# One block's x transposed by DMA instead of by TensorE, and its neighbour's V loaded from GpSimd's queue, in a fused chunk attention and squared-ReLU feed-forward kernel

## The chip, the cores and the metric

The kernel runs on one core of a Trainium2 chip. The metric is the device time of one execution in microseconds (us); a kernel's figure is the median over its runs. Besides the plain times there is one profiled execution, whose trace gives the engines' instructions in order of time.

## The reference

Attention inside chunks of 64 tokens, for 8 batches, 8 heads, 576 tokens and head size 64, and after it a feed-forward layer with a squared ReLU on the 4608 rows of 512 that the attention gives.

```python
# q, k, v: (8, 8, 576, 64) float32, cut into chunks of 64 tokens
scores = scale * np.matmul(q_c, k_c.transpose(0, 1, 2, 4, 3))
attn = exp(scores - max) ; attn = attn / (sum(attn) + 1e-09)
x = np.matmul(attn, v_c)              # then laid out as (4608, 512)
h = np.maximum(x @ w_in, 0.0)         # w_in: (512, 2048)
out = (h * h) @ w_out                 # w_out: (2048, 512), out float32
```

## The kernel before

Tokens are worked in 18 groups of 256 (four chunks each), and two groups make a block of 512 tokens: nine blocks, 0 to 8. Block 4 is groups 8 and 9, block 5 is groups 10 and 11, block 6 is groups 12 and 13. The whole order of the work is written out by hand: every step is put into a numbered slot, and the engines execute what they are given in that order.

**Attention of a group.** q and k of a group are loaded into a staging buffer by three DMAs on SyncE's queue (SP), two for k and one for q (`qk_pieces`, L266 and L279). `C`, made of `CQ` and `CK` (L449, L454), casts them to bfloat16 into `qkb`, on GpSimd for block 5. `TD` (`transpose_qk_dma`, L460) transposes `qkb` into `qkT` with one DMA on SP. `SC` (`scores`, L483 and L494) does 32 small matmuls and one Exp on ScalarE. `AV` (`values`, L510) multiplies with V, in two tiles, and VectorE divides by the row sums and writes the tile of `x` (L442, L443). V of a group is loaded by DMAs on SP (`v_pieces`, L308 for the even heads, L312 for the odd ones): five for group 10, four for group 11. `XT` (`transpose_x`) brings x into `xT`, tokens along the free dimension: with eight TensorE transposes into a PSUM bank and a copy by ScalarE (L540, L545), or, for the blocks in `X_BY_DMA`, with one DMA transpose on SP (L535). PSUM banks for attention are handed out in turn by `att_bank`, two of them in this stage.

**Feed-forward.** Blocks 0 to 3 have a plain first product, `ffn_in`: 16 slots, each with four matmuls of 128x512 (L579), a ReLU on ScalarE (L590) and a square on VectorE (L598), or on ScalarE for slots 3, 10 and 14. The squares are the pieces of `gT`. From block 4 on the first product is done by a Strassen-like scheme of seven products per quarter block (`quad_step`, L657, steps A1, B2, A6, C5, A7, C3, A4), which needs four sums of x, `x_sums` 0 to 3, called e1 to e4 below. VectorE forms them (L614). e1 is made of two parts of group 8 alone; e2 is e1 plus a part of group 9, e3 is e2 minus a part of group 9, and e4 is made of parts of both. A1 reads e1, A6 reads e2, C5 reads e3, A4 reads e4.

The second product (`ffn_out`) has the same kind of scheme, with the differences d4, d5, d2 and d3 of `gT` pieces formed by VectorE (L614, written to `w_st`). For block 3 it is a generator: d4 is formed in two halves in input slots 14 and 15, and then come 14 output steps of eight matmuls (L780): two of the product p2, which reads `gT` itself, two of p1, which reads d4, then two with d5, and so on. d5 is formed after the third output step.

**Around the change.** Block 3's input stage (`j == 3` in the loop over `QUADS`) holds, beside its 16 x 4 matmuls: `SC` of groups 8 and 9 in slot 2, `AV` of group 8 in slot 6 and of group 9 in slot 10, the loads for block 5 (one per slot in slots 0 to 10), the casts of group 10 in slot 11, the cast of q of group 11 and `TD` of group 10 in slot 13, `XT` of group 8 in slot 13 and of group 9 in slot 15. The first `LEAD` = 4 output steps of block 3 then run before the first quarter of block 4, with `between[n]` executed after n of them: `CK` and `TD` of group 11 and one more load before the first, one load after each of the next three, and the x sums. Then block 4's quarters interleave with the other ten output steps, `SC` of group 10 at 1.5, `SC` of group 11 at 3.5, and the four `AV` tiles of block 5 at 4.5, 6, 7.5 and 10 (a unit is one pair of products).

SP executes its DMA instructions in order. In the program as built, each DMA of SP also waits until the one eight before it on SP has landed, and the same holds on GpSimd's queue (eight semaphores in turn on either). GpSimd's queue holds, in order: the casts for block 5, a store of an output tile (L809), then two squares of block 4's products (L676).

Of the kernel before, what the change touches and what calls it, by code (L numbers as in the profile page):

```python
# [144 lines left out]
def kernel(  # L145
# [34 lines left out]


    FIRST_DMA_T = 4
    X_BY_DMA = (6, 7, 8)
    QUADS = 4
    LEAD = 4

# [60 lines left out]
    def runs(g):  # L247

        for t in range(2):
            (b, s), (b1, s1) = chunks[g][2 * t:2 * t + 2]  # L250
            if b == b1:
                yield t, 0, 2 * CH, b, s
            else:
                yield t, 0, CH, b, s
                yield t, CH, CH, b1, s1
# [48 lines left out]
    def v_pieces(g):  # L304

        even, odd = [], []
        for t, p, m, b, s in runs(g):
            even.append(lambda t=t, p=p, m=m, b=b, s=s: nc.sync.dma_start(  # L308
                out=v_even[g % NV][p:p + m, t, :, 0:D],
                in_=v[b, 0::2, s:s + m, :].rearrange("h s d -> s h d")))  # L310
        for n, p, m, b, s in odd_loads[g]:
            odd.append(lambda n=n, p=p, m=m, b=b, s=s: nc.sync.dma_start(  # L312
                out=v_odd[n % NO][p:p + m, :, 0:D],
                in_=v[b, 1::2, s:s + m, :].rearrange("h s d -> s h d")))
        if g < 2:
            yield from [even[0], *odd[:-1], even[1], odd[-1]]
        else:
            yield from even + odd

    def go(pieces):  # L320
        for f in pieces:
            f()
# [604 lines left out]
    def pieces(grps):  # L927
        for g in grps:
            yield from qk_pieces(g)
        for g in grps:  # L930
            yield from v_pieces(g)
# [72 lines left out]
    for j in range(QUADS):  # L1004
        grps, nxt, far = blocks[j], blocks[j + 1], blocks[j + 2]
        plan = {}

        def at(slot, f, *x):
            plan.setdefault(slot, []).append((f, x))

        if j == 0:
            loads, go_slots = pieces(far), range(17)
            at(28, summed(b11_p_b21, b11, b21))
            for slot, f in ((24, TA), (27, SC), (29, AV), (31, XT)):
                at(slot, f, nxt[0])
            at(31, TQ, nxt[1])
            at(31, TK, nxt[1])
            at(31, summed(b22_m_b21, b22, b21, ALU.subtract))
            phases = [first_ffn_in, ffn_out_by_ft(0)]
        elif j == 1:  # L1020
            loads, go_slots = itertools.chain(*map(qk_pieces, far)), range(26, 48)
            for slot, f in ((3, SC), (6, AV), (12, XT)):
                at(slot, f, grps[1])
            for i, g in enumerate(nxt):
                for slot, f in ((16 + 4 * i, C), (21 + 4 * i, TD), (36 + i, SC), (38 + 2 * i, AV),
                                (41 + 2 * i, XT)):
                    at(slot, f, g)
            for i, g in enumerate(far):
                at(36 + 4 * i, C, g)
                at(42 + 3 * i, TD, g)  # L1030
            at(2, summed(b12_p_b21, b12, b21))
            at(12, summed(b11_m_b12, b11, b12, ALU.subtract))
            at(20, summed(b12_p_b22, b12, b22))
            out_j = ffn_out(1)
            for i in (20, 27, 29, 31):
                at(i, lambda: next(out_j)())
            phases = [ffn_in(1, [(0, 256, FT_ORDER), (256, 256, FT_ORDER)]), out_j]
        else:
            out_j = ffn_out(j)
            for i in (14, 15):  # L1040
                at(i, lambda: next(out_j)())
            phases = [ffn_in(j, [(0, BT, range(n_ft))])]
            if j == 2:
                loads, go_slots = itertools.chain(*map(v_pieces, nxt), pieces(far)), [
                    *range(16), *range(27, 36)]
                slots = {SC: (6, 10), AV: (12, 22), XT: (15, 28), CQ: (20, 22), CK: (21, 24), TD: (24, 26)}
                for f in (CQ, CK, TD):
                    for i, g in enumerate(far):
                        at(slots[f][i], f, g)
                phases.append(out_j)  # L1050
            else:
                loads, go_slots = pieces(far), range(11)
                at(11, C, far[0])
                at(13, CQ, far[1])
                at(13, TD, far[0])
                slots = {SC: (2, 2), AV: (6, 10), XT: (13, 15)}
            for f in (SC, AV, XT):
                for i, g in enumerate(nxt):
                    at(slots[f][i], f, g)
            if j == 2:  # L1060
                for i, f in enumerate((summed(a21_p_a22, a21, a22),
                                       summed(a12_m_a21, a12, a21, ALU.subtract),
                                       summed(a11_p_a21, a11, a21))):
                    at(1 + 2 * i, f)
        slot = 0
        for phase in phases:
            for _ in phase:
                if slot in go_slots:
                    for f in loads:
                        f()  # L1070
                        break
                for f, x in plan.get(slot, []):
                    f(*x)
                slot += 1
        assert all(x < slot for x in plan), (j, slot, sorted(plan))
        if j < QUADS - 1:
            go(loads)
# [19 lines left out]
    for j in range(QUADS, n_blk):  # L1097
        if j == QUADS:
            n = 14 - LEAD
            slots = [1 + 19 * i // n for i in range(n)]  # L1100
            assert len(slots) == n
        else:
            slots = [s for s in range(4, 20) if s % 16 not in NO_OUT]
            start = 3
        if j == QUADS:
            g = blocks[QUADS + 1][1]
            between = {0: [(CK, (g, nc.scalar.copy)), (TD, (g,))]}
            for n in (0, 1, 2, 3):
                between.setdefault(n, []).append((load, (1, loads)))
            for n in (2, 2, 2, 3):  # L1110
                between.setdefault(n, []).append((x_sums, (QUADS, len([1 for z in between.values() for y in z if y[0] is x_sums]))))
            for f, x in between.get(0, []):
                f(*x)
            for i in range(LEAD):
                next(out_j)
                tock()
                for f, x in between.get(i + 1, []):
                    f(*x)
        else:
            outs[j - 1] = ffn_out(j - 1)  # L1120
            at(j, start, lambda j=j: next(outs[j - 1])())
        for s in slots:
            plan.setdefault(("out", 16 * (j - QUADS) + s), []).append(outs[j - 1])

        if j + 1 < n_blk:
            S0, V0, V1, X0 = ((1.5, 3.5), (4.5, 7.5), (6, 10), (8.5, 12)) if j == QUADS else (
                (1.5, 7), (3.5, 8), (5, 9.5), (5.5, 10)) if j == QUADS + 1 else (
                (0.5, 7), (2, 8), (3.5, 9.5), (3.5, 10)) if is_whole(blocks[j + 1][0]) else (
                (3.5, 9.5), (5, 11), (7, 12), (8, 13))
            for i, g in enumerate(blocks[j + 1]):  # L1130
                at(j, S0[i], SC, g)
                at(j, V0[i], AV0, g)
                at(j, V1[i], AV1, g)
                at(j, X0[i], XT, g)
            if j + 2 == n_blk:
                at(j, 22, check_sums)
                at(j, 25.5, count_bad)
            for i, s in enumerate((13.5, 16 if j == n_blk - 3 else 15, 17.5, 18)):
                at(j, s, x_sums, j + 1, i)
        if j == QUADS:  # L1140
            for s in range(4):
                at(j, 4 * s + 2, w_sums_in_place, s)
            assert next(loads, None) is None
        if j + 2 < n_blk:
            more = pieces(blocks[j + 2])
            if j == n_blk - 3:

                for s, n in ((0, 1), (1, 1), (2, 1), (8.5, 3), (13, 5), (15, 2), (15.5, 2)):
                    at(j, s, load, n, more)
            else:  # L1150
                for s in range(0, 16):
                    at(j, s, load, 1 if is_whole(blocks[j + 2][0]) else 2, more)
            for i in range(2):
                at(j, (9, 10 if j == QUADS else 13)[i], C, blocks[j + 2][i])
                at(j, ((9.5, 14.5) if j == n_blk - 3 else (12, 13.5))[i], TD, blocks[j + 2][i])
# [66 lines left out]
```

## Time and profile before

| | us |
|---|---|
| runs of the kernel | 277.05, 277.80, 279.23 (median 277.80) |
| the profiled execution | 276.91 |
| its span in the trace | 275.1 |
| VectorE busy | 199.2 |
| ScalarE busy | 168.3 |
| GpSimd busy | 89.6 |
| median issue to landing, q of a group (512 KB) | 5.6 |
| the same, V for 128 rows (128 KB) | 3.9 and 3.6 |

The profiled execution is 1.8 us longer than its span, the part that lies outside of the trace's first and last instruction, and 0.9 us below the median of the three runs. The granted TensorE clock is full in every stretch of the span. In the listings, PE is TensorE's matmuls, PEld its weight loads, DVE VectorE, ACT ScalarE, POOL GpSimd, SP SyncE, and SPq what SP spends on issuing DMAs.

### The profile page before, as it was taken

The numbers are of one execution on the slowest core, as the hardware profiler recorded it, in microseconds if no ns is written. First come the engines' busy times: TensorE is split into PE (matmuls) and PEld (weight loads), VectorE is DVE, ScalarE is ACT, GpSimd is POOL, SyncE is SP. The second block draws the span as 40 slices with busy tenths as digits, with TensorE's granted clock in tenths as the row PEclk, the third lists the DMA queues.
The fourth block names the chain that finished last, engine by engine and source line by source line (L and its number), as shares of the span: only waits on it lengthen the run. The fifth ranks groups of instructions, "written<-read, shape, count | busy, mean of one in ns | idle before, by whom it ended". The sixth has DMA issues, their size and how long they took to land.

```text
span 275.1 us, 7923 instructions
## 1 busy us (share of the span) xinstructions
PE 264.9 (96%) x3261; PEld 203.4 (74%) x3261; DVE 199.2 (72%) x365; ACT 168.3 (61%) x300; POOL 89.6 (33%) x122
## 2 busy tenths in 40 slices
PE   2999999999999999999999999999999999999995
PEld 2764445888774588447878888888888888888884
DVE  1457514999538592499989998799779877994752
ACT  1657614894458883877678765565746665756430
POOL 2048834240360012040245224551643212331600
PEclk9999999999999999999999999999999999999999
DMA  7999999999999999999999999697999530220223
GB/s 216 262 352 389 361 332 270 339 213 172 262 210 218 238 234 218 275 223 178 228 236 197 218 238 194 103 220 196 244 187 224 123 76 2 99 55 7 71 83 114
DMA packets 136056, 55.60 MB, mean 202 GB/s; under 512 B 104273, under 2 KB 131921, under 8 KB 136017
## 3 DMA queue, kind: packets, MB, share of 16 engines
q1 hardware_dynamic: 133248, 46.54, 74.0%
q0 software_dynamic: 2624, 8.39, 9.6%
q8 instruction: 26, 0.43, 0.6%
q10 hardware_dynamic: 144, 0.13, 0.1%
q14 instruction: 14, 0.11, 0.1%
HBM read 36.70 MB, written 9.44 MB: 168 GB/s over the span
## 4 chain that ended last, share of the span: by engine, by line
PE 87%; DMA 4%; SPq 3%; DVE 3%; ACT 1%; issue 1%; ACTq 0%; DVEq 0%
PE ps_ffn L657 22%; PE ps_out L780 22%; PE ps_ffn L579 17%; PE ps_ffn L780 14%; PE ps_ffn L901 5%; PE ps_att L510 3%; PE ps_att L540 2%; DMA vo_sb<-in_v_dram 2%; PE ps_att L483 2%; DMA xT<-x 2%; DVE gT L598 2%; SPq L266 1%; SPq L308 1%; SPq L312 1%; DVE x L443 1%; ACT e L494 1%
## 5 line engine op out<-in xcount | busy, mean ns | idle before, releaser
L579 PE MATMUL ps_ffn<-xT,w_in_bf 128*128 128x512 bf16 (+1 forms) x328 | 57.8, 333 | 0.0
L780 PEld LDWEIGHTS <-w_st 128*128 128x128 bf16 x512 | 48.9, 98 | 6.6 <-DVE w_st L614 0.5
L665 DVE CUSTOM_DVE_ANT_0 relu<-ps_ffn,w_st 128x512 f32<-128x512 f32 x60 | 39.3, 684 | 13.0 <-PE ps_ffn L657 11.6
L579 PEld LDWEIGHTS <-w_in_bf 128*128 128x128 bf16 x328 | 31.2, 98 | 21.6 <-POOL w_in_bf L334 0.2
L598 DVE TENSOR_TENSOR gT<-relu 128x256 bf16<-128x256 bf16 (+2 forms) x68 | 34.1, 537 | 17.8 <-ACT relu L590 17.3
L590 ACT ACTIVATE relu<-ps_ffn 128x256 bf16<-128x256 f32 (+2 forms) x82 | 39.4, 501 | 9.4 <-PE ps_ffn L579 8.6
L657 PE MATMUL ps_ffn<-qk_st,w_in_bf 128*128 128x256 bf16 x240 | 35.3, 273 | 0.1
L657 PEld LDWEIGHTS <-w_in_bf 128*128 128x128 bf16 x320 | 30.7, 98 | 4.1 <-issue 0.3
L809 POOL DMA_DIRECT2D out_dram<-o_sb x24 | 17.6, 733 | 43.6 <-DVE o_sb L614 23.3
L780 PEld LDWEIGHTS <-gT 128*128 128x128 bf16 x296 | 28.6, 98 | 3.3
L780 PE MATMUL ps_out<-w_out_bf,w_st 128*128 128x256 bf16 x240 | 30.8, 273 | 0.0
L699 ACT ACTIVATE w_st<-ps_ffn 128x512 f32<-128x512 f32 x20 | 11.9, 597 | 29.6 <-PE ps_ffn L657 29.6
L443 DVE TENSOR_TENSOR x<-ps_att,recs 128x512 bf16<-128x512 f32 x36 | 24.9, 692 | 1.2
L657 PEld LDWEIGHTS <-qk_st 128*128 128x128 bf16 x240 | 22.6, 98 | 3.2 <-DVE qk_st L614 0.3
L657 PE MATMUL ps_ffn<-xT,qk_st 128*128 128x256 bf16 x160 | 23.9, 273 | 0.0
L676 POOL TENSOR_TENSOR qk_st<-relu 128x512 bf16<-128x512 f32 x10 | 10.3, 1034 | 41.6 <-DVE relu L665 38.1
L494 ACT ACTIVATE e<-ps_att 128x1024 bf16<-128x1024 f32 x18 | 18.3, 1025 | 8.5 <-PE ps_att L483 8.5
L676 POOL TENSOR_TENSOR gT<-relu 128x512 bf16<-128x512 f32 x10 | 10.3, 1033 | 35.4 <-DVE relu L665 30.5
L449 POOL CAST qkb<-qk_st 128x1024 bf16<-128x1024 f32 x12 | 13.0, 1082 | 14.9 <-DMA qk_st<-in_q_dram 14.9
L674 ACT ACTIVATE gT<-relu 128x512 bf16<-128x512 f32 x28 | 17.7, 631 | 0.0
L780 PE MATMUL ps_ffn<-w_out_bf,w_st 128*128 128x256 bf16 x144 | 17.7, 273 | 0.0
L614 DVE TENSOR_TENSOR w_st<-gT,w_st 128x1024 bf16<-128x1024 bf16 x26 | 16.8, 682 | 0.0
(92 smaller groups left out, 428.7 us busy)
## 6 DMA issues: line engine op xcount, KB each, us to landing
qk_st<-in_q_dram SPq DMA_DIRECT2D x16, 512.0 KB, 5.6
out_dram<-o_sb POOLq DMA_DIRECT2D x28, 256.0 KB, 3.9
qk_st<-in_k_dram SPq DMA_DIRECT2D x24, 256.0 KB, 5.6
ve_sb<-in_v_dram SPq DMA_DIRECT2D x32, 128.0 KB, 3.9
w_st<-in_moe_w_in_dram SPq DMA_DIRECT2D x8, 512.0 KB, 5.9
w_st<-in_moe_w_out_dram SPq DMA_DIRECT2D x8, 512.0 KB, 5.5
vo_sb<-in_v_dram SPq DMA_DIRECT2D x24, 128.0 KB, 3.6
qk_st<-in_k_dram SPq DMA_DIRECT2D x4, 512.0 KB, 5.8
```

The costliest lines, as they stand in the source:

```text
L443: nc.vector.tensor_tensor(out=x, in0=o[:, :, :, 0:D], in1=rec.to_broadcast([128, 2, n, D]), op=ALU.mult)
L494: nc.scalar.activation(out=e_out, in_=s_in, func=AF.Exp, scale=scale)
L579: nc.tensor.matmul(out=h[:, 0:n], lhsT=w_in_bf[:, dt, ft * 128:(ft + 1) * 128], rhs=xT[:, c // 128:(c + n) // 128, dt, :], start=(dt == 0) ...
L590: nc.scalar.activation(out=rl[:, 0:n], in_=h[:, 0:n], func=AF.Relu)
L598: nc.vector.tensor_tensor(out=dst, in0=src, in1=src, op=ALU.mult)
L614: nc.vector.tensor_tensor(out=out, in0=in0, in1=in1, op=op)
L657: nc.tensor.matmul(out=bank[:, f * GT:(f + 1) * GT], lhsT=a[:, dt, ft * 128:(ft + 1) * 128], rhs=b[:, :, dt, :], start=(first and f == 0 a ...
L665: nc.vector._custom_dve(TENSOR_ADD_SAT, out=out, in0=in0, in1=in1, s0=BIG, s1=0.0)
L674: engine.activation(out=dst, in_=r, func=AF.Square)
L676: engine.tensor_tensor(out=dst, in0=r, in1=r, op=ALU.mult)
L780: nc.tensor.matmul(out=out_ps, lhsT=lhsT, rhs=b[:, i, :], start=(first and i == 0 and (last or t == 0)), stop=(i == HF - 1), skip_group_ch ...
L809: dma.dma_start(out=out[t0:t0 + GT, col:col + HD].rearrange("(t p) d -> p t d", p=128), in_=o_sb.rearrange("p (t d) -> p t d", d=HD))
```

## The change

Three edits.

1. Block 4 joins the blocks whose x is transposed by DMA on SP. `XT` of group 8 moves from slot 13 to slot 8 of block 3's input stage and `XT` of group 9 from slot 15 to slot 11; `TD` of group 10 moves from slot 13 to slot 12.
2. V of groups 10 and 11 (block 5) is issued by GpSimd on its own queue, no longer by SP: the five of group 10 together in slot 13, behind the cast of q of group 11; the four of group 11 where their issues stood before, through `between`. The loads of slots 0 to 5 are the six of q and k, as before.
3. Of the four x sums of block 4, e1 stays after the second output step of block 3; e2 and e3 move to after the third, where e4 already was. On VectorE this puts them behind the two instructions of d5.

In the built program TensorE has 32 instructions fewer (16 weight loads and 16 transposes, L540), ScalarE two copies fewer (L545), SP nine V loads fewer and two transposes more, GpSimd nine DMA issues more.

```diff
     FIRST_DMA_T = 4
-    X_BY_DMA = (6, 7, 8)
+    V_BY_GPSIMD = (10, 11)
+    X_BY_DMA = (4, 6, 7, 8)
...
     def v_pieces(g):
 
         even, odd = [], []
+        dma = nc.gpsimd if g in V_BY_GPSIMD else nc.sync
         for t, p, m, b, s in runs(g):
-            even.append(lambda t=t, p=p, m=m, b=b, s=s: nc.sync.dma_start(
+            even.append(lambda t=t, p=p, m=m, b=b, s=s: dma.dma_start(
                 out=v_even[g % NV][p:p + m, t, :, 0:D],
                 in_=v[b, 0::2, s:s + m, :].rearrange("h s d -> s h d")))
         for n, p, m, b, s in odd_loads[g]:
-            odd.append(lambda n=n, p=p, m=m, b=b, s=s: nc.sync.dma_start(
+            odd.append(lambda n=n, p=p, m=m, b=b, s=s: dma.dma_start(
...
             else:
-                loads, go_slots = pieces(far), range(11)
+                loads, go_slots = pieces(far), range(6)
                 at(11, C, far[0])
+                at(12, TD, far[0])
                 at(13, CQ, far[1])
-                at(13, TD, far[0])
-                slots = {SC: (2, 2), AV: (6, 10), XT: (13, 15)}
+                at(13, lambda: go(itertools.islice(loads, 5)))
+                slots = {SC: (2, 2), AV: (6, 10), XT: (8, 11)}
...
-            for n in (2, 2, 2, 3):
+            for n in (2, 3, 3, 3):
                 between.setdefault(n, []).append((x_sums, (QUADS, ...
```

The branch that `XT` of block 4 now takes is already in the kernel before:

```python
        if g // 2 in X_BY_DMA:
            nc.sync.dma_start_transpose(out=dst, in_=x.rearrange("p t h a d -> p (t h a d)"))
            return
```

## The prediction

> **What bounds the kernel now.** I read the page first, then the chain of waits, then the timeline of block 3's input stage and of the first 20 us behind it. The page:
>
> ```profile
> span 275.1 us, 7923 instructions
> PE 264.9 (96%) x3261; PEld 203.4 (74%) x3261; DVE 199.2 (72%) x365; ACT 168.3 (61%) x300; POOL 89.6 (33%) x122
> PE 87%; DMA 4%; SPq 3%; DVE 3%; ACT 1%; issue 1%; ACTq 0%; DVEq 0%
> ```
>
> TensorE (PE) is busy for 96% of the span and carries 87% of the chain, so removed TensorE work should shorten the kernel, unless TensorE then waits at the same place. The chain of waits through the stage that is changed (start, length, what):
>
> ```profile
> 115.70 1.90 DVE gT L598 x3
> ...
> 119.28 2.78 DVE gT L598 x3
> 122.21 0.70 DVE x L443
> 122.96 0.62 PE ps_att L540 x8
> ```
>
> From 115.70 on VectorE carries the chain, and the eight transposes of group 8 (L540) come off it at 122.96: their PSUM bank is free only when x of group 9's first tile has been read. One square among these is slow; the first row is VectorE's groups from 120.8 to 121.6, the second GpSimd's cast of k of group 10 in the timeline:
>
> ```profile
> L598 DVE TENSOR_TENSOR gT<-relu 128x512 bf16<-128x512 f32 x1 | 1.5, 1519 | 0.0
> 120.21 1.30 POOL L454 CAST qkb<-qk_st 128x1024 bf16<-128x1024 f32 x1 [0.74 <-DMA qk_st<-in_k_dram]
> ```
>
> The timeline of the same place, TensorE first and then VectorE (start, length, instructions; idle before it in brackets):
>
> ```profile
> 120.08 2.76 PE L579 MATMUL ps_ffn<-xT,w_in_bf 128*128 128x512 bf16 x12
> 123.42 1.89 PE L579 MATMUL ps_ffn<-xT,w_in_bf 128*128 128x512 bf16 x8
> 125.14 0.61 PE L540 MATMUL ps_att<-ident,x 128*128 128x128 bf16 x8
> 125.59 1.91 PE L780 MATMUL ps_out<-w_out_sum,gT 128*128 128x256 bf16 x16
> 127.34 1.94 PE L780 MATMUL ps_out<-w_out_bf,w_st 128*128 128x256 bf16 x16
> 129.11 0.60 PE L657 MATMUL ps_ffn<-qk_st,w_in_bf 128*128 128x256 bf16 x4
> ```
>
> ```profile
> 123.05 0.69 DVE L443 TENSOR_TENSOR x<-ps_att,recs 128x512 bf16<-128x512 f32 x1
> 123.66 1.89 DVE L598 TENSOR_TENSOR gT<-relu 128x512 bf16<-128x512 f32 x3
> 125.46 0.68 DVE L614 TENSOR_TENSOR w_st<-gT 128x1024 bf16<-128x1024 bf16 x1
> 126.31 0.69 DVE L598 TENSOR_TENSOR gT<-relu 128x512 bf16<-128x512 f32 x1 [0.17 <-ACT relu L590]
> 127.04 0.69 DVE L614 TENSOR_TENSOR w_st<-gT 128x1024 bf16<-128x1024 bf16 x1
> 127.65 0.42 DVE L614 TENSOR_TENSOR qk_st<-xT 128x512 bf16<-128x512 bf16 x1
> 128.98 1.28 DVE L614 TENSOR_TENSOR w_st<-gT,w_st 128x1024 bf16<-128x1024 bf16 x2
> ```
>
> VectorE has one idle piece of 0.17 us there. The row at 127.04 is the second half of d4, and ends at 127.73. Product p1 (127.34) reads that half from its fifth matmul on: p1 takes 129.11 - 127.34 = 1.77 us for 16, so the fifth starts at 127.34 + 4 x 0.111 = 127.78. TensorE is 0.05 us behind VectorE already.
>
> **Transposes removed from TensorE and ScalarE.** Eight matmuls take (125.14 - 123.42) = 1.72 us up to the second eight transposes, which fill 125.14 to 125.59 (0.45 us). Without transposes slots 14 and 15 follow slot 13 directly: 120.08 + 12 x 0.215 = 122.66, and 1.72 us later, at 124.4, p2 starts instead of at 125.59. TensorE gains 1.2 us by then: 0.3 us of wait and twice 0.45 us.
>
> That gain meets VectorE. Its instructions are the same and in the same order up to e1, and those up to 126.1 had no idle time to lose. The last ReLU comes earlier (its matmuls end at 124.4), so only the 0.17 us before 126.31 goes, 0.24 us with the gap in the issue. The second half of d4 ends at about 127.5, and p1's fifth matmul, which TensorE could reach at 124.4 + 1.75 + 0.44 = 126.6, waits until 127.55. Twelve matmuls later, 127.55 + 1.33 = 128.9, comes A1, at 129.11 before: **0.2 us gained** of 1.2. ScalarE's two copies had nothing behind them that sets the end but this ReLU, and so are worth nothing more.
>
> The slow square (1.52 us, where the three from 123.66 take 0.63 each) lies beside that cast. The loads of q and k and the cast stay where they are, so I leave this time in.
>
> **x sums.** VectorE after the change: d4 to 127.5, e1 (0.42) to 127.9, d5 (1.28) to 129.2, e2 and e3 to 130.1. TensorE needs e1 at 128.9, d5 at 129.7, e2 for A6 at 130.6 (0.2 us before its old 130.86). Each is early by 0.5 to 1 us, the total is the same: zero, as long as the xT of group 9 lands by 129.2.
>
> **The two transposes on SP.** SP's rows, and the time that each kind of transpose takes to issue and to land (min/median/max):
>
> ```profile
> 118.21 1.73 SPq L279 DMA_DIRECT2D qk_st<-in_k_dram  x2
> 124.36 5.15 SPq L460 DMA_TRANSPOSE qkT<-qkb  x2
> L535 SPq DMA_TRANSPOSE xT<-x x6: 1233/1555/2757, 162.7 to 223.9; - x6
> DMA to landing us min/median/max: 3.0/4.6/5.5
> L460 SPq DMA_TRANSPOSE qkT<-qkb x14: 1317/3058/4518, 61.7 to 206.3; - x14
> DMA to landing us min/median/max: 4.5/6.1/8.5
> ```
>
> x of group 8 is ready at 119.28 (the chain) and SP free at 118.21 + 1.73 = 119.94: landing at 122.9 to 125.4, e1 reads it at 127.5. x of group 9 is ready at 123.05 + 0.69 = 123.74: its transpose is issued at 123.8 and lands at 126.8 to 129.3, at 128.4 by the median; e2 reads it at 129.2. Both hidden, the second by 0.8 us. Behind it on SP stands `TD` of group 10, whose casts were done long before: issued at 123.8 + 1.55 = 125.4, 1.0 us later than before. `TD` of group 11 follows at up to 128.4 (before, the second of the two rows waited for a cast that the copies on ScalarE held up). Who waits for them:
>
> ```profile
> 131.39 0.45 PE L483 MATMUL ps_att<-qkT 64*64 64x64 bf16 x32
> 134.05 0.45 PE L483 MATMUL ps_att<-qkT 64*64 64x64 bf16 x32
> 136.28 0.22 PE L510 MATMUL ps_att<-ve_sb,e 64*64 64x65 bf16 x2
> 140.07 0.22 PE L510 MATMUL ps_att<-ve_sb,e 64*64 64x65 bf16 x2
> ```
>
> Scores of group 10 now come at 131.2, 5.8 us after the issue; of group 11 at 133.8, 5.4 us after it. By the minimum (4.5) both are hidden, by the median (6.1) they cost 0.3 and 0.7 us, by the maximum 3. Here the V loads no longer stand ahead of `TD` on SP, so I take a landing of 5 to 5.5 us and a cost of zero, with 0 to 3.1 us for the range.
>
> **V on GpSimd.** Nine issues behind the cast of q of group 11, ahead of a store and a square:
>
> ```profile
> 122.01 1.04 POOL L449 CAST qkb<-qk_st 128x1024 bf16<-128x1024 f32 x1 [0.50 <-DMA qk_st<-in_q_dram]
> 131.50 0.71 POOL L809 DMA_DIRECT2D out_dram<-o_sb  x1 [8.45 <-DVE o_sb L614]
> 131.71 1.28 DVE L614 TENSOR_TENSOR w_st<-gT 128x1024 bf16<-128x1024 bf16 x2
> 135.83 1.04 POOL L676 TENSOR_TENSOR qk_st<-relu 128x512 bf16<-128x512 f32 x1 [3.62 <-DVE relu L665]
> L809 POOL DMA_DIRECT2D out_dram<-o_sb x24: 707/738/751, 69.9 to 239.0; - x24
> DMA to landing us min/median/max: 2.2/3.6/6.0
> ```
>
> No V load is issued there before. The nearest row is a store, 0.74 us for 256 pieces of 1 KB. A V load has 512 pieces of 256 B (two of the nine have half): by bytes no more than the store, by pieces 1.48 us. Nine take 6.6 us or 7 x 1.48 + 2 x 0.74 = 11.8 us, from 123.05 to between 129.7 and 134.9; even then the store (0.71) ends at 135.6, before the square's 135.83. The fifth load is issued by 129.0 and lands by 135.0 at the slowest row (6.0); `AV` needs it at 136.1. The ninth lands by 139.4 in the same way, group 11's `AV` is at 139.9. Cost zero, thinly covered at the slow end. If an issue held up VectorE as the cast did (0.9 us), the four to six issues that lie before d4's end would cost some 4 to 5 us; but VectorE beside a store (131.71, two in 1.28 us) is not slowed at all, and a V issue is nearer to a store than to a cast.
>
> SP loses the nine issues (five of them fill 119.94 to 124.36) and gains two of 1.55 us, so block 6's loads start 1 to 3 us earlier. One wait later on could profit, the 0.20 us before this:
>
> ```profile
> 206.62 0.61 PE L657 MATMUL ps_ffn<-qk_st,qk_st 128*128 128x256 bf16 x4 [0.20 <-DVE qk_st L614]
> ```
>
> I count half of it. Sum: -0.2 - 0.1 = -0.3 us, a span of 274.8. The profiled execution takes 276.91, 1.8 outside its span, and lies 0.9 below the median 277.8. Median to median: **277.5**.
>
> **Rivals.** *TensorE's whole gain arrives:* 277.8 - 1.2 - 0.1 = 276.5. It needs VectorE's 12 us from 115.70 to 127.73 to shrink by 1 us, for instance if the cast no longer meets the square (0.9 us). Against it: nothing in the change moves that cast.
>
> *Transposes late, the slow side:* `TD` of groups 10 and 11 land more than 5.8 and 5.4 us after their issue, because V now runs at the same time from another queue instead of ahead of them, and two more transposes are in flight. TensorE executes in order, so each tenth beyond is lost. 6.1 us gives 277.5 + 0.7 = 278.2; 8.5 us gives 277.5 + 3.1 = 280.6 (the second wait holds the first). For it: the median of 14 landings is already beyond the point. Against it: the scores rows at 131.39 and 134.05 show no wait for a DMA, though V stood ahead of both on the same queue. [...]
>
> [...]
>
> That the transposes stay on TensorE is no rival: the built program has 16 fewer.
>
> **Numbers.** The forecast has 0.56, TensorE's whole gain 0.12, late transposes 0.25, starved V 0.07. A median of this kernel can't be told from no change within about 1%, 275.0 to 280.6. The forecast and the whole gain lie inside but for spread (runs of one kernel span 277.05 to 279.23): faster 0.04. Slower takes starved V and a quarter of the late transposes: 0.13. Same 0.83. The range goes from the whole gain with 0.3 of spread, 276.2, to late transposes at 279.8.
>
> **What would show it.** Right: no L540 after 115, p2 near 124.4, a wait of 0.9 us in p1 for VectorE, A1 near 128.9, scores of groups 10 and 11 without a wait for DMA, V issues of 0.7 to 1.5 us on POOL. Wrong: L443 or L598 ending earlier than in the rows above (more gain), PEld waiting on qkT at L483 (slower), a square L676 later than 136.

## The result and the profile after

| | before | after |
|---|---|---|
| median of six runs each on one chip, us | 277.78 (277.05 to 279.23) | 283.73 (279.72 to 289.86) |
| profiled execution, us | 276.91 | 281.77 |
| its span, us | 275.1 | 280.0 |

The ratio is 1.013, with a 95% interval of 1.009 to 1.017: slower, by about 1.3%. It is lower than that of the medians (1.021) because the comparison leaves out executions that lie over 1.5% above a kernel's fastest, and here the change makes such executions itself, as the granted clock will show. The forecast was 277.5, in a range of 276.2 to 279.8.

In the kernel after, lines from `v_pieces` on stand two further down: `TD` is L462, the DMA of `XT` L537, `SC` L485, the V loads L310 and L314, squares L600, VectorE's sums L616, A1 and its like L659, the output products L782. The page of after:

```profile
span 280.0 us, 7901 instructions
PE 265.7 (95%) x3242; PEld 203.4 (73%) x3245; DVE 199.6 (71%) x365; ACT 167.0 (60%) x298; POOL 96.5 (34%) x131
PEclk9999999999999999999799999999999999999999
PE 76%; DVE 10%; DMA 7%; SPq 3%; ACT 1%; issue 1%; ACTq 0%; DVEq 0%
```

TensorE has lost 11 points of the chain to VectorE (3% to 10%) and the DMAs (4% to 7%). It has 16 transposes fewer and yet 0.8 us more busy time: the twentieth slice of the clock row, the one with the 7 (133 to 140 us), is the reason. Where the DMA comes in, the chain of waits says (start, length, what):

```profile
119.39 3.48 DVE gT L600 x3
...
125.90 8.81 DMA qkT<-qkb
```

`TD` of group 10 is in the chain with 8.81 us. TensorE's timeline over the same place:

```profile
124.48 1.91 PE L782 MATMUL ps_out<-w_out_sum,gT 128*128 128x256 bf16 x16
127.01 0.61 PE L782 MATMUL ps_out<-w_out_bf,w_st 128*128 128x256 bf16 x4 [0.62 <-DVE w_st L616]
128.34 1.48 PE L782 MATMUL ps_out<-w_out_bf,w_st 128*128 128x256 bf16 x12 [0.72 <-DVE w_st L616]
129.66 0.60 PE L659 MATMUL ps_ffn<-qk_st,w_in_bf 128*128 128x256 bf16 x4
...
134.76 0.45 PE L485 MATMUL ps_att<-qkT 64*64 64x64 bf16 x32 [2.75 <-DMA qkT<-qkb]
...
138.83 0.63 PE L485 MATMUL ps_att<-qkT 64*64 64x64 bf16 x32
```

p2 starts at 124.48, 1.1 us earlier than before. The brackets in the next two rows give that away again: p1 waits for VectorE, and A1 comes at 129.66, 0.55 us later than before. Then the scores of group 10 wait 2.75 us for `TD`. They start 3.37 us later than before (134.76 against 131.39), those of group 11 4.78 us later (138.83 against 134.05). The span is 4.9 us longer, so from there on nothing more is lost. The two scores rows stand 4.07 us apart, in before 2.66, and no wait lies between them: the windows of TensorE show why (PE, PEld, DVE, ACT and POOL busy, then the granted clock, DMA share, GB/s).

```profile
134.00:135.00 1.00, 0.24 (x28) 0.24 (x32) 1.00 (x3) 0.00 (x0) 0.00 (x0) 1.00 1.28 228
135.00:136.00 1.00, 1.00 (x36) 0.88 (x21) 1.00 (x3) 0.73 (x1) 0.00 (x0) 0.95 1.29 381
136.00:137.00 1.00, 1.00 (x7) 0.69 (x6) 0.00 (x0) 0.92 (x3) 0.00 (x0) 0.50 0.98 307
...
138.00:139.00 1.00, 1.00 (x17) 0.48 (x18) 0.00 (x0) 0.59 (x1) 0.00 (x0) 0.50 1.27 288
```

About 1 us after the wait has ended the clock falls to 0.50, until 139.3 or so. So the profiled execution's 4.9 us are 0.55 up to A1, 2.82 from A1 to the scores of group 10 (2.75 in the row's wait for `TD`), and 1.4 at the low clock.

What ran while `TD` was under way: GpSimd's timeline, and the landing times of `TD` (the view of one line: issue min/median/max and where, then issue to landing). The first pair of rows is group 10's alone, the second both groups'.

```profile
122.27 1.50 POOL L310 DMA_DIRECT2D ve_sb<-in_v_dram  x2
...
127.34 1.37 POOL L314 DMA_DIRECT2D vo_sb<-in_v_dram  x2
```

```profile
L462 SPq DMA_TRANSPOSE qkT<-qkb x1: 4107/4107/4107, 125.9 to 125.9; - x1
...
DMA to landing us min/median/max: 8.8/8.8/8.8
L462 SPq DMA_TRANSPOSE qkT<-qkb x2: 3753/3930/4107, 125.9 to 130.1; - x2
...
DMA to landing us min/median/max: 6.9/7.9/8.8
```

All nine V loads are issued between 122.3 and 128.7. `TD` of group 10, issued among them at 125.9, lands after 8.8 us (4.8 before), that of group 11 after 6.9 (4.5 before). The issue itself takes 4.1 us of SP in place of 3.0, so group 11's goes out at 130.1 only.

### The profile page after: what moved, and what is told of

Read it like the earlier page. It is cut to its first block, busy times and chain, and to the rows that moved or that the text cites. A ratio compares the mean times of both kernels' runs of the same rounds, so it can differ in the third digit from the quotient of the medians.

```text
span 280.0 us, 7901 instructions
## 1 busy us (share of the span) xinstructions
PE 265.7 (95%) x3242; PEld 203.4 (73%) x3245; DVE 199.6 (71%) x365; ACT 167.0 (60%) x298; POOL 96.5 (34%) x131
## 4 chain that ended last, share of the span: by engine, by line
PE 76%; DVE 10%; DMA 7%; SPq 3%; ACT 1%; issue 1%; ACTq 0%; DVEq 0%
PE ps_ffn L659 22%; PE ps_out L782 21%; PE ps_ffn L782 11%; PE ps_ffn L581 11%; DMA qkT<-qkb 5%; PE ps_ffn L903 5%; DVE gT L600 5%; PE ps_att L512 2%; DMA vo_sb<-in_v_dram 2%; PE ps_att L485 2%; DVE x L445 1%; SPq L267 1%; PE ps_att L542 1%; SPq L310 1%; DVE w_out_bf L616 1%
## 5 line engine op out<-in xcount | busy, mean ns | idle before, releaser
L782 PEld LDWEIGHTS <-w_st 128*128 128x128 bf16 x512 | 48.7, 98 | 8.4 <-DVE w_st L616 2.4
L600 DVE TENSOR_TENSOR gT<-relu 128x256 bf16<-128x256 bf16 (+2 forms) x68 | 33.5, 527 | 19.0 <-ACT relu L592 18.7
L659 PE MATMUL ps_ffn<-qk_st,w_in_bf 128*128 128x256 bf16 x240 | 36.1, 278 | 0.1
L659 PEld LDWEIGHTS <-w_in_bf 128*128 128x128 bf16 x320 | 31.1, 99 | 4.5 <-issue 0.3
L782 PE MATMUL ps_out<-w_out_bf,w_st 128*128 128x256 bf16 x240 | 31.0, 273 | 1.3 <-DVE w_st L616 1.3
L782 PEld LDWEIGHTS <-gT 128*128 128x128 bf16 x296 | 28.7, 98 | 3.5
L678 POOL TENSOR_TENSOR qk_st<-relu 128x512 bf16<-128x512 f32 x10 | 10.3, 1033 | 45.7 <-DVE relu L667 40.3
L659 PEld LDWEIGHTS <-qk_st 128*128 128x128 bf16 x240 | 22.8, 99 | 3.4 <-DVE qk_st L616 0.3
L659 PE MATMUL ps_ffn<-xT,qk_st 128*128 128x256 bf16 x160 | 24.4, 277 | 0.0
L678 POOL TENSOR_TENSOR gT<-relu 128x512 bf16<-128x512 f32 x10 | 10.3, 1034 | 35.2 <-DVE relu L667 34.8
L451 POOL CAST qkb<-qk_st 128x1024 bf16<-128x1024 f32 x12 | 13.4, 1115 | 15.5 <-DMA qk_st<-in_q_dram 15.5
L782 PE MATMUL ps_ffn<-w_out_bf,w_st 128*128 128x256 bf16 x144 | 17.6, 273 | 0.0
L616 DVE TENSOR_TENSOR w_st<-gT,w_st 128x1024 bf16<-128x1024 bf16 x26 | 16.8, 682 | 0.0
```

Of the source, the lines that this page charges most:

```text
L600: nc.vector.tensor_tensor(out=dst, in0=src, in1=src, op=ALU.mult)
L616: nc.vector.tensor_tensor(out=out, in0=in0, in1=in1, op=op)
L659: nc.tensor.matmul(out=bank[:, f * GT:(f + 1) * GT], lhsT=a[:, dt, ft * 128:(ft + 1) * 128], rhs=b[:, :, dt, :], start=(first and f == 0 a ...
L678: engine.tensor_tensor(out=dst, in0=r, in1=r, op=ALU.mult)
L782: nc.tensor.matmul(out=out_ps, lhsT=lhsT, rhs=b[:, i, :], start=(first and i == 0 and (last or t == 0)), stop=(i == HF - 1), skip_group_ch ...
```

## The experiments

Theory A: a DMA transpose on SP lands late while plain transfers that another queue issued are in flight. Its rivals put the delay down to the two added transposes on SP, to the order on SP, or to GpSimd. Theory C: TensorE's idle time costs a second time, because the granted clock falls after it. All edits are made to the kernel after unless it says otherwise; a ratio is to the kernel before on the same chip, with its 95% interval.

**V left out.** The loads of V of block 5 are not issued by any queue; block 5 is multiplied with older contents of V's buffers.

```diff
-        if g < 2:
+        if g in V_BY_GPSIMD:
+            yield from [lambda: None] * len(even + odd)
+        elif g < 2:
```

> The changed kernel without the nine V loads of block 5 (block 5 then multiplies with the V that its buffers held before). Theory A, other queue: TD of group 10 took 8.8 us to land because the V loads from GpSimd's queue ran at the same time. Then it lands within 5 to 6 us, at about 131.5, the scores of group 10 wait less than 0.5 us, the clock stays full, and the time is 276.5 to 278. Theory B, order on SP: TD was late because it stands behind x of group 9's transpose and two transposes were added. Then it still takes 8 us or more, the wait of 2.7 us stays, and the time stays at 281 to 284.

Measured: median 277.86, ratio 0.999 (0.994 to 1.003). The whole loss is gone, with both added transposes in place. The view of `TD` (L464 here), both transposes:

```profile
L464 SPq DMA_TRANSPOSE qkT<-qkb x2: 1836/2088/2341, 129.8 to 131.7; - x2
...
DMA to landing us min/median/max: 4.5/4.7/4.9
```

Landing 4.5 and 4.9 us, issue 1.8 and 2.3; the scores have no wait and start at 135.08 and 137.75, 2.67 us apart. (The stage lies some 3 us later in this execution, which had a low clock of its own at 72 to 76 us, ahead of the changed stage.) Two more transposes on SP are not what delays `TD`.

**V on GpSimd alone.** The other two edits are undone.

```diff
-    X_BY_DMA = (4, 6, 7, 8)
+    X_BY_DMA = (6, 7, 8)
-                at(12, TD, far[0])
+                at(13, TD, far[0])
-                slots = {SC: (2, 2), AV: (6, 10), XT: (8, 11)}
+                slots = {SC: (2, 2), AV: (6, 10), XT: (13, 15)}
-            for n in (2, 3, 3, 3):
+            for n in (2, 2, 2, 3):
```

> The kernel before with one part of the change: V of block 5 from GpSimd's queue (its loads where the changed kernel has them); x of block 4 by TensorE and the x sums as before. Theory A, other queue: TD of group 10, issued at about 123 to 125 beside the V loads, takes 7 to 9 us, the scores of group 10 wait about 1 us or more, and the time is 279 to 281. Theory B, order on SP: TD lands in 4.5 to 6 us, no wait, 277 to 278.

Measured: median 280.68, ratio 1.005 (1.000 to 1.011). `TD` lands after 7.2 us (group 10, issued early enough at 121.5) and 7.0 us (group 11). The rows of group 11, of `TD` and of TensorE:

```profile
L462 SPq DMA_TRANSPOSE qkT<-qkb x1: 3407/3407/3407, 128.8 to 128.8; - x1
...
DMA to landing us min/median/max: 7.0/7.0/7.0
```

```profile
135.87 0.45 PE L485 MATMUL ps_att<-qkT 64*64 64x64 bf16 x32 [1.15 <-DMA qkT<-qkb]
```

So V on the other queue slows `TD` by itself. The wait is at group 11's scores, not at group 10's as I expected. It costs less than in the whole change, because one `TD` is issued early enough; the added transposes took that lead.

**x by DMA alone.** V of block 5 goes back to SP, five loads behind `TD` of group 10 and four behind that of group 11.

```diff
-    V_BY_GPSIMD = (10, 11)
+    V_BY_GPSIMD = ()
```

> The changed kernel with V of block 5 back on SP: the five loads of group 10 right behind TD of group 10, the four of group 11 behind TD of group 11. Theory A, other queue: TD of group 10 lands in 5 to 6 us, the scores of group 10 wait less than 0.5 us; TD of group 11 now stands behind five V issues and may wait instead; 277 to 280. Theory B, order on SP: TD of group 10 takes 8 us or more as in the changed kernel, wait 2.7 us, 281 to 284.

Measured: median 281.85, ratio 1.015 (1.007 to 1.024). SP's timeline and the scores of group 11:

```profile
126.00 1.83 SPq L462 DMA_TRANSPOSE qkT<-qkb  x1
127.88 1.70 SPq L310 DMA_DIRECT2D ve_sb<-in_v_dram  x2
129.62 1.82 SPq L314 DMA_DIRECT2D vo_sb<-in_v_dram  x3
131.55 4.00 SPq L462 DMA_TRANSPOSE qkT<-qkb  x1
```

```profile
137.42 0.45 PE L485 MATMUL ps_att<-qkT 64*64 64x64 bf16 x32 [3.32 <-DMA qkT<-qkb]
```

`TD` of group 10 is issued at the same time as in after (126.0) and lands after 4.3 us instead of 8.8: no wait. `TD` of group 11 now stands behind five V issues, goes out at 131.55, lands after 5.8, and TensorE waits 3.32 us. The kernel is about as slow as after, beyond the 280 us that I expected at most, for another reason, its order on SP. That speaks for A; and it shows that taking V off SP did save SP's time, which was then paid back beside the transposes.

**TD of group 10 before the second x.**

```diff
-                at(12, TD, far[0])
+                at(11, TD, far[0])
```

> The changed kernel with TD of group 10 one slot earlier, so that on SP it stands ahead of the transpose of x of group 9 and need not wait for that x. Both theories: TD is issued at about 122 and lands by 130.5, the scores of group 10 do not wait. Theory A, other queue: it takes 7 to 8.5 us to land even so, and the transpose of group 9's x lands later than 129.2, so that VectorE waits for it. Theory B, order on SP: it lands in 4.5 to 6 us. Time 276.5 to 279 by either.

Measured: median 287.23 (282.45 to 291.78, four runs; no ratio). VectorE's timeline:

```profile
135.77 0.89 DVE L616 TENSOR_TENSOR qk_st<-qk_st,xT 128x512 bf16<-128x512 bf16 x2 [6.86 <-DMA xT<-x]
```

I expected 276.5 to 279 us and it is the slowest of all: as theory A had it, the second xT is the late transpose (issued at 126.9, landed after 8.8 us), and the two `TD` take 10.3 and 11.0, where A had 7 to 8.5. All three transposes issued from 123.4 on, beside the V loads, are late; the other order only moved TensorE's wait, from 2.75 us at the scores to 5.59 us at e2.

**V from GpSimd, earlier.** All nine V loads are issued in slot 3, ahead of the block's loads of q and k in time.

```diff
-                loads, go_slots = pieces(far), range(6)
+                loads, go_slots = itertools.chain(*map(qk_pieces, far)), range(6)
-                at(13, lambda: go(itertools.islice(loads, 5)))
+                at(3, lambda: go(itertools.chain.from_iterable(map(v_pieces, far))))
```

> The changed kernel with all nine V loads of block 5 issued by GpSimd in slot 3 of block 3's input stage, ahead of the casts, so that they run before the transposes. Theory A, V beside the transposes is what makes them late: the transposes land in 3 to 4.7 us (x) and 4.3 to 6 us (TD), no wait at the scores of groups 10 and 11 over 0.5 us, full clock, 277 to 278 us. Rival, the added transposes load the engines whatever V does and V only shifts the load: q and k of block 5 land some 3 us later beside V, the casts and TD follow, and the scores wait again by 1 us or more: 279 to 281.

Measured: median 279.68, ratio 1.005 (1.002 to 1.007). The transposes, now without V beside them, land in time, and VectorE's d4 is slow:

```profile
L462 SPq DMA_TRANSPOSE qkT<-qkb x2: 1847/2238/2630, 129.1 to 131.1; - x2
...
DMA to landing us min/median/max: 4.6/4.7/4.9
```

```profile
125.33 1.52 DVE L616 TENSOR_TENSOR w_st<-gT 128x1024 bf16<-128x1024 bf16 x1
```

Most of the loss is gone, as A says, but not all: 277 to 278 us were expected. What stays is another cost, and half of the rival: V beside the loads of q and k on SP delays those. The first four of them land after 8.4 to 10.6 us (5.2 to 5.6 in x by DMA alone), and the issues of two k and one q take 5.0 and 4.5 us. So it is not transposes alone that are late beside another queue's loads. GpSimd's casts (123.2 to 128.4) then fall on d4, whose first half takes 1.52 us instead of 0.68, and p1 waits 2.1 us for it in two pieces, 0.64 us and this one:

```profile
128.95 2.74 PE L782 MATMUL ps_out<-w_out_bf,w_st 128*128 128x256 bf16 x12 [1.43 <-DVE w_st L616]
```

The twelve matmuls take 2.74 us, 1.48 in after: here too the clock falls to 0.50, from 128.8 to 132.2, at the end of the second of these short pauses. Four of the ten executions have such a mean clock (0.994); the six others have 0.999 or 1.000 and are at 278.18 to 280.05 us, so the clock is not alone what keeps this kernel above the one before (median 278.22 on this chip).

**V from ScalarE.**

```diff
-        dma = nc.gpsimd if g in V_BY_GPSIMD else nc.sync
+        dma = nc.scalar if g in V_BY_GPSIMD else nc.sync
```

> The changed kernel with the nine V loads of block 5 issued by ScalarE instead of GpSimd, at the same places of the program. Theory A1, any second queue with plain loads holds the transposes up: TD takes 7 to 9 us to land as before. Theory A2, only GpSimd's queue does: TD lands in 4.5 to 6 us. The time itself mixes in what the issues cost ScalarE (some 0.5 us each, nine of them, in front of its ReLUs): 279 to 284 by A1, 277.5 to 280 by A2.

Measured: median 283.45, ratio 1.020 (1.014 to 1.026). Group 10's `TD`:

```profile
L462 SPq DMA_TRANSPOSE qkT<-qkb x1: 3925/3925/3925, 125.4 to 125.4; - x1
...
DMA to landing us min/median/max: 7.3/7.3/7.3
```

```profile
128.47 0.69 DVE L600 TENSOR_TENSOR gT<-relu 128x512 bf16<-128x512 f32 x1 [2.07 <-ACT relu L592]
```

With six V issues from ScalarE between 122.6 and 127.8, group 10's `TD` takes 7.3 us; group 11's, issued at 130.0 in a pause of V (one load still in flight at its start, one issued before its end), takes 4.3. So it is not GpSimd as the issuer. The time is lost elsewhere in this kernel: the issues stand in front of the last ReLU on ScalarE, VectorE waits 2.07 us for it, TensorE 2.88 us for VectorE, A1 comes at 131.34, the clock is at 0.50 from 131.2 to 138.0, and the scores have no wait.

**Work in TensorE's pause.** 46 matmuls of 128x128 on the identity, without use, stand in front of the scores of group 10 (TensorE's lines stand five further down).

```diff
+            if j == QUADS:
+                at(j, 1.5, busy_bank, 46)
             for i, g in enumerate(blocks[j + 1]):
                 at(j, S0[i], SC, g)
```

> The changed kernel with 46 matmuls of 128x128 on the identity (2.6 us by the 0.45 us that eight of them take) put in front of the scores of group 10, where TensorE waited 2.75 us for TD; their result is not used. Theory C, the wait costs more than itself because the clock falls to half behind it: TD still lands in 8 to 9 us, the clock stays full, the scores of groups 10 and 11 stand 2.7 us apart again instead of 4.1, and the time falls by 1 to 1.5 us, to 280 to 282.5, with less spread between the runs. Rival, the clock falls for another reason than the idle time: it falls here too, and the time stays at 282 to 285.

Measured: median 281.73 (after: 283.73), ratio 1.015 (1.010 to 1.021). The median is 2 us lower, the ratio is no lower than that of after; what decides is the profile. TensorE's timeline:

```profile
130.85 2.73 PE L440 MATMUL ps_att<-ident 128*128 128x128 bf16 x46
134.59 0.45 PE L490 MATMUL ps_att<-qkT 64*64 64x64 bf16 x32 [1.00 <-DMA qkT<-qkb]
...
137.25 0.45 PE L490 MATMUL ps_att<-qkT 64*64 64x64 bf16 x32
```

`TD` of group 10 is as late (8.8 us; the trace has no landing of group 11's), but with a pause of 1.00 us instead of 2.75 the clock is 1.000 over the whole span, and the scores are 2.66 us apart as in before, 4.07 in after. Theory C holds for the profiled execution: 1.4 us of after's loss are the clock. Of the four executions of this kernel three have the full clock, of after's six one. One of the three takes 282.67 us, so the clock is not the whole spread.

**The x sums back.**

```diff
-            for n in (2, 3, 3, 3):
+            for n in (2, 2, 2, 3):
```

> The changed kernel with e2 and e3 back after the second output step. If the move is what the prediction said, cover for the landing of group 9's transpose: e2 waits for it from about 128.6 to 130.2, d5 ends at about 132.3 instead of 129.8, and TensorE's first product with d5 waits 1 to 2 us; the scores of group 10 wait that much less for TD, so that the time is 0 to 1 us longer than the changed kernel's. If the move does nothing, all places stay within 0.3 us.

Measured: median 282.67, ratio 1.014 (1.008 to 1.021). TensorE's timeline:

```profile
130.23 1.21 PE L782 MATMUL ps_out<-w_out_sum,w_st 128*128 128x256 bf16 x8 [0.55 <-DVE w_st L616]
...
136.87 0.55 PE L485 MATMUL ps_att<-qkT 64*64 64x64 bf16 x32 [4.99 <-DMA qkT<-qkb]
```

With e2 ahead of d5, VectorE waits 1.08 us for the second xT, and TensorE 0.55 us for d5. I had expected 1 to 2 us. The move of the sums is worth that half microsecond, which the late `TD` (11.5 and 9.8 us here) hides.

**V on SP in its old order.** The five loads of group 10 stay in slots 6 to 10, on SP among and ahead of the transposes; group 11's four behind the last one.

```diff
-    V_BY_GPSIMD = (10, 11)
+    V_BY_GPSIMD = ()
-                loads, go_slots = pieces(far), range(6)
+                loads, go_slots = pieces(far), range(11)
-                at(13, lambda: go(itertools.islice(loads, 5)))
```

> V of block 5 goes back to SP's queue and into the order of the kernel before: five loads of group 10 between the last load of k and the transposes, four of group 11 behind the last transpose. The two transposes of x stay on the DMA. Theory A (transposes are slow only while plain transfers of another queue run beside them): the two xT land within 6 us of their issue, the two qkT too, no wait for them at the scores (0 to 0.3 us), TensorE's first ffn product of the output stage 0.3 to 0.5 us earlier against VectorE's squares than in the kernel before, median 277 to 278, ratio 0.997 to 1.002. Rival (two more transposes on SP make the next ones late, whatever else runs): one of the scores waits 1 us or more, ratio 1.006 to 1.015. The second qkT is issued behind five V loads and two xT, at about 127.5, and has until 133.8, which is the thin place.

Measured: median 278.28, ratio 1.002 (0.999 to 1.005). The view of `TD`, and TensorE's timeline:

```profile
L462 SPq DMA_TRANSPOSE qkT<-qkb x2: 1949/2272/2594, 127.8 to 129.9; - x2
...
DMA to landing us min/median/max: 4.4/5.0/5.6
```

```profile
132.32 0.45 PE L485 MATMUL ps_att<-qkT 64*64 64x64 bf16 x32 [0.31 <-DMA qkT<-qkb]
...
135.53 0.45 PE L485 MATMUL ps_att<-qkT 64*64 64x64 bf16 x32 [0.48 <-DMA qkT<-qkb]
```

The four transposes stay on SP and the loss is gone, with landings as A expects. Only the waits are 0.3 and 0.5 us instead of nothing, and A1 is late (129.66), not early as I expected, since the three squares took 3.56 us beside the casts as in after. Its span is 276.5.

**The same, and one square moved from VectorE.** In block 3's input stage ScalarE squares tiles 3, 6, 8 and 10.

```diff
-            if (n == 512 and ft in SQUARES_ON_ACT) or (
+            if (n == 512 and ft in (SQUARES_ON_ACT if j < 3 else (3, 6, 8, 10))) or (
```

> As sp_order, and in block 3's input stage ScalarE computes the squares of tiles 3, 6, 8 and 10 in place of 3, 10 and 14, so VectorE has one square (0.63 us) less and the last ReLU comes 0.6 us earlier. If the step holds that VectorE's chain to the second half of d4 takes what TensorE would gain, the wait of the first product for VectorE shrinks from some 0.7 us to 0.3 or less and the time falls by another 0.3 to 0.6 us: 276.5 to 277.3, ratio 0.995 to 0.998. If something else holds TensorE there, it equals sp_order.

Measured: median 278.05, ratio 1.001 (0.998 to 1.003). Its profiled execution (288.06 us) lost time elsewhere, above all to a wait of 4.44 us for an earlier `TD` at 75 us and a low clock from 73 to 80, so only the rows of the stage are read, where the clock is 1.00:

```profile
131.49 1.91 PE L782 MATMUL ps_out<-w_out_sum,gT 128*128 128x256 bf16 x16
...
134.19 1.48 PE L782 MATMUL ps_out<-w_out_bf,w_st 128*128 128x256 bf16 x12 [0.36 <-DVE w_st L616]
135.52 0.60 PE L659 MATMUL ps_ffn<-qk_st,w_in_bf 128*128 128x256 bf16 x4
```

From p2 to A1 it takes 4.03 us. In after it takes 5.18, but with two squares slowed by casts; in x by DMA alone, with one as here, 4.34. In before, where p2 comes later, it takes 3.52. VectorE's chain is what holds TensorE there, as the prediction had it. In the medians the expected 0.3 to 0.6 us can't be told from nothing.

**The transposes drawn ahead of V on SP,** with the same squares: first xT, three V loads, `TD` of group 10, second xT, `TD` of group 11, six V loads.

```diff
-                at(13, lambda: go(itertools.islice(loads, 5)))
+                at(9, lambda: go(itertools.islice(loads, 3)))
-                at(12, TD, far[0])
+                at(11, TD, far[0])
-                between.setdefault(n, []).append((load, (1, loads)))
+                between.setdefault(n, []).append((load, (2 - n // 2, loads)))
```

> From sp_order_sq, with the order on SP changed: the first transpose of x stands right behind the last load of k, then three V loads of group 10, the first qkT (group 10), the second transpose of x, the second qkT (group 11), and the other six V loads behind it. In sp_order the two qkT were issued at 127.8 and 129.8 and the scores waited 0.31 and 0.48 us for them. By theory A (alone in time, a transpose lands 3.3 to 6 us after its issue) both qkT are issued 2 us earlier and nothing waits at the scores; the second xT lands 0 to 0.5 us late for the second sum. With the shorter wait for VectorE that makes 276.9 to 277.7, ratio 0.996 to 0.999. Rival (V loads issued behind the transposes catch them up): the second qkT lands 7 us or more after its issue, 278 to 280.

Measured: median 279.57, ratio 1.002 (0.998 to 1.005); not the gain I expected. Both `TD` land after 4.3 and 4.5 us and nothing waits at the scores. But SP came to the first xT at 122.2, 2.1 us after x, and the second xT is issued at 130.0:

```profile
133.84 0.61 PE L659 MATMUL ps_ffn<-qk_st,qk_st 128*128 128x256 bf16 x4 [1.58 <-DVE qk_st L616]
```

The wait has moved to e2. None of the versions beats the kernel before by anything that its spread would let one see.

## Why the prediction was wrong

**The step that failed** is "The two transposes on SP", with its sentence "Here the V loads no longer stand ahead of `TD` on SP, so I take a landing of 5 to 5.5 us and a cost of zero". Measured were 8.8 and 6.9 us. I took V's leave from SP as a relief, where it turned V from work ahead of `TD` into work beside it. All kernels in one table (us from issue to landing, in the order of the groups):

| | V of block 5 | xT, groups 8 and 9 | `TD` 10 | `TD` 11 | wait at the scores, 10 and 11 |
|---|---|---|---|---|---|
| before | SP | TensorE | 4.8 | 4.5 | none |
| V left out | none | 4.5 and 3.4 | 4.5 | 4.9 | none |
| x by DMA alone | SP | 4.7 and 3.4 | 4.3 | 5.8 | 0, 3.32 |
| V on SP, old order | SP | 3.3 (one seen) | 4.4 | 5.6 | 0.31, 0.48 |
| the same, one square moved | SP | 4.0 and 3.5 | 4.5 | 4.3 | 0.28, 0 |
| transposes drawn ahead | SP | 5.3 and 3.3 | 4.5 | 4.3 | none |
| V earlier | GpSimd, before them | 4.6 and 3.4 | 4.6 | 4.9 | none |
| V on GpSimd alone | GpSimd, beside | TensorE | 7.2 | 7.0 | 0, 1.15 |
| after | GpSimd, beside | 4.4 and 5.6 | 8.8 | 6.9 | 2.75, 0 |
| work in the pause | GpSimd, beside | 4.6 and 6.1 | 8.8 | not in the trace | 1.00, 0 |
| sums back | GpSimd, beside | 4.9 and 5.0 | 11.5 | 9.8 | 4.99, 0 |
| `TD` first | GpSimd, beside | 6.1 and 8.8 | 10.3 | 11.0 | 0, 0 (5.59 at e2) |
| V from ScalarE | ScalarE, beside `TD` 10 | 4.8 and 5.9 | 7.3 | 4.3 | none |

Not one `TD` here without V beside it takes over 5.8 us, none with four or more of V's loads beside it under 6.9. The transposes of x, half as much data, suffer less: up to 6.1 us, and 8.8 only where a `TD` beside V stands ahead. The trace of before gave a sign of this. In the view of `TD`, the median of 6.1 that I quoted mixes two kinds. These rows are of before, GpSimd's stores (from its timeline), and the `TD` issued beside each:

```profile
196.42 0.75 POOL L809 DMA_DIRECT2D out_dram<-o_sb  x1
...
206.23 1.47 POOL L809 DMA_DIRECT2D out_dram<-o_sb  x2
```

```profile
L460 SPq DMA_TRANSPOSE qkT<-qkb x1: 4518/4518/4518, 196.5 to 196.5; - x1
...
DMA to landing us min/median/max: 8.5/8.5/8.5
```

```profile
L460 SPq DMA_TRANSPOSE qkT<-qkb x1: 3532/3532/3532, 206.3 to 206.3; - x1
...
DMA to landing us min/median/max: 8.3/8.3/8.3
```

Of the 14, six have a store issued between 1.5 us before them and 2 us after: 7.4, 6.0, 5.1, 7.3, 8.5 and 8.3 us. The eight others take 4.5 to 6.5, half of them under 5. These limits are drawn after the fact and one of the six is not late, so it is a sign and not a rule. But for a `TD` among nine loads from GpSimd it made a price above 5.8 us likelier than one of 5 to 5.5, and with it the rival "transposes late" likelier than the forecast.

**The rival** had the cause right (a chance of 0.25; `TD` takes 8.8 and 6.9 us with V on the other queue, 4.5 and 4.9 without V), and "6.1 us gives 278.2; 8.5 us gives 280.6" was too small. It left out that the clock fell to 0.50 after the pause of 2.75 us (1.4 us in the profiled run, more in others: the six runs of after have 279.72 us at a mean clock of 1.000, 281.77 to 284.07 at 0.993 or 0.994, 286.18 at 0.988, 289.86 at 0.980), and it had `TD` issued at 125.4, where it was 125.90. "A quarter of the late transposes" for slower by over 1% was too little by the same count.

**TensorE's gain** ends at VectorE, as worked out: p2 at 124.48 (124.4 predicted), a wait of 1.34 us in p1 for d4 (0.9 predicted). A1 was to come at 128.9 and came at 129.66. The step held the slow square fixed, since "the loads of q and k and the cast stay where they are". It is not fixed. In after the casts ran at 119.42 to 122.3, two squares are slow (1.52 us each) instead of one, and the three take 3.56 us in the timeline, 2.86 in before. The run with work in TensorE's pause, the same program as after up to the scores, has one slow square:

```profile
119.15 2.73 DVE L605 TENSOR_TENSOR gT<-relu 128x512 bf16<-128x512 f32 x3
```

So where the casts fall differs between executions, and the change does not decide it. From the start of the three squares at 115.7 to A1 it takes 13.4 us in before; 13.0 in four kernels with one slow square (work in the pause, x by DMA alone, `TD` first, sums back), and 13.85 in three with two (after, V left out, V on SP in its old order). The term of -0.2 is -0.4 or +0.45. In after it made no difference in the end: with work in the pause A1 comes 1.0 us earlier, at 128.67, and the scores of group 10 at 134.59 instead of 134.76, since the landing of `TD` sets their place. That VectorE is the bound, the run with a square less confirms.

**The x sums:** the cost of zero was nearly right; e2 waited 0.41 us for the second xT, and A6 behind it did not. **V on GpSimd:** an issue takes 0.75 us, like the store's and not twice as much by pieces, nine take 6.5 us; no store, square or `AV` came late for it, nor was VectorE held up. "Starved V" is out: no run shows the term behind its chance of 0.07 (also counted into "slower"), that VectorE holds up an issue; the nine took 0.63 to 0.75 us each, with VectorE busy for 6.90 of the 7 us from 122 to 129. **SP's lighter load** (-0.1 us) did not come about: the two `TD` hold SP until 133.9, and block 6's first load goes out 1.0 us later than before (133.92 against 132.88), not 1 to 3 us earlier. TensorE stays 4.8 to 4.9 us behind to the end.

What stays open is in which execution the clock falls. It goes with TensorE's pauses in this stage. Where the profile shows one of 2.75 us or more (after, x by DMA alone, sums back, `TD` first, V from ScalarE), 19 of 22 executions have a mean granted clock below 0.997. Where the longest is 1.0 to 1.6 us (V on GpSimd alone, V earlier, work in the pause, transposes drawn ahead), 9 of 36 have it; where none is over 0.8 us (before with 72 executions, V left out, V on SP in its old order and with one square moved), 4 of 107. But the length alone does not decide: in the profile of V earlier 0.64 and 1.43 us sufficed, in that of x by DMA alone 3.32 us did not. The low stretches last 3.4 us (135.9 to 139.3 in after) or twice that (134.3 to 141.1 in `TD` first). What decides beside the length was not shown: no run here moved the pause alone.

## What to carry to other kernels

Don't price a transfer by the median over a trace: sort its landings by what other queues had in flight, and take the price of the class that the change will put it in. V moved to another queue took nine issues (7.4 us in before) off SP and put V's bytes beside the transposes: `TD` of group 10 landed after 8.8 us in place of 4.8. So keep a DMA on which the busiest engine waits clear of another queue's loads. And to a wait of TensorE of some 3 us add what the clock may take after it, 1.4 us in the profile of after; in one profile it fell after pauses of 0.64 and 1.43 us already, in another not after 3.32 us.

## What the runs showed of the hardware

- A DMA transpose of 256 tokens of q and k took 4.3 to 5.8 us with plain loads ahead of or behind it on its own queue, and 6.9 to 11.5 us with four or more loads of up to 128 KB in flight from another, GpSimd's or (7.3) ScalarE's. Its issue on SP grew too, from 1.8 and 2.3 us in the kernel without V to 4.1 and 3.8 in after, where group 11's so went out at 130.1; but behind five V loads on SP itself it took 4.0 us as well (x by DMA alone).
- Plain loads took longer too. V landed in a median of 4.7 to 5.0 us beside the transposes in after, in 3.0 on SP behind them (x by DMA alone) and 4.0 to 4.2 on SP in its old order; loads of q and k on SP beside V from GpSimd landed in 8.4 to 10.6 us (V earlier), without it in 5.2 to 5.6 (x by DMA alone) and 5.1 to 6.8 (before).
- An issue on GpSimd took 0.75 us for 512 pieces of 256 B and 0.63 us for 256 of them (after), and 0.74 us for 256 pieces of 1 KB (the median of 24 stores in before).
- Beside a GpSimd cast, the first half of d4 took 1.52 us (V earlier; 0.68 in before), and a square 1.52 us (one in before, two in after; 0.63 to 0.69 otherwise). Beside GpSimd's DMA issues both kept their time (0.69 in after).
- In the five profiles in which the clock fell in this stage, it stayed at 0.50 for 3.4 us (after, V earlier, sums back) or 6.8 us (`TD` first, V from ScalarE).
